# Cosine attention and a low-rank mixer with an MLP on one core: the combined blocks of the second MLP weight are built one unit earlier, in buffers that attention gives up

## The chip, the core and the metric

The kernel runs on one core of a Trainium2 chip. The metric is device time in microseconds (us); lower is better. TensorE (PE) multiplies matrices, VectorE (DVE), ScalarE (ACT) and GpSimd (POOL) work on elements, SyncE (SP) only starts transfers, as POOL does too. Every engine works through its own instructions strictly in the order in which they were written, and waits where an operand isn't ready.

## The reference

Inputs are q, k, v of 8 batches, 12 heads, 448 positions and 64 features. After the attention, its output is laid out as x with 448 rows and 768 columns for each batch:

```python
q_n = q / (norm(q) + 1e-06); k_n = k / (norm(k) + 1e-06)
attn = softmax(q_n @ k_n.T / tau)
x = (attn @ v).transpose(0, 2, 1, 3).reshape(B, S, H * D)
u = x + (x.T @ U @ V).T            # U: 448 x 32, V: 32 x 448
out = u + relu(u @ w_ch1) @ w_ch2  # w_ch1: 768 x 3072, w_ch2: 3072 x 768
```

The rest of this text calls the two weights w1 and w2. Multiplying by w1 is "up", multiplying by w2 is "down".

## The kernel before

**Tokens and units.** Two batches have 896 rows of u, which are seven tiles of 128 rows; four pairs of batches give 28 tiles. The MLP takes them in units. `PLAIN = [3, 4, 3, 4]` says that the first four units take 3, 4, 3 and 4 tiles and multiply in the ordinary way (`mlp`): up is 24 blocks of w1 times 6 steps, each a matmul of 128 columns per tile (L1294), then down is, for each tile and each half of the output columns, 24 matmuls of 384 columns (L1330). The other 14 tiles go in seven units of two tiles (`mlp_seven`). There, down uses seven block products in the place of eight: w2 is cut in 2 x 2 blocks, four combined blocks (`seven_weights`, L1014: T1, T2, T4, and one written over a block of w2) and as many combinations of the hidden values (`sums_of`, L1169 to L1172: S1, S2, an overwritten Q block, and S4) are formed by DVE subtractions, and each of seven products is 12 matmuls of 384 columns (L1217). The products are joined by DVE additions (L1233), one copy by ACT (L1238) and three additions by POOL (L1240). With `HALF = 2`, the first two of these seven units do an ordinary up for two tiles (24 x 6 matmuls of 256 columns, L1188), and the last five do up with seven products as well (`up_seven`, L1087, 252 matmuls of 128 columns), after `seven_rows` (L1046 to L1049) has formed combined blocks of w1.

**Attention** of batch b+1 and later runs beside the MLP units of earlier batches. For each batch, three loads of q and k (POOL's queue, L529) bring four heads each; DVE or ACT squares them (L581, L577), DVE sums (L585) and normalises (L653), SP starts transposing transfers (L668), PE forms scores (L714), ACT takes exponentials (L732), PE multiplies with v (L759), DVE divides into X (L788, L790). `stage0` then makes u from X: a projection (L866), a matmul with V (L921), and DVE additions of X (L931, L939). For batches from 2 on, u goes to DRAM (L964). A unit reads it back twice, transposed into uT (L816) and plain (L820).

**Buffers.** Rings hand out buffers in turn. Loads of q and k have 3 buffers (`r_ld`), normalised values 3 (`r_xn`), squares 3 (`r_sq`), transposed q and k 6 (`r_qkT`), projections 3 (`r_A`), u 4 for making (`r_us`) and 4 for reading back (`r_ur`). T1 and T2 lie over the load buffers and T4 over v of even batches and over the squares, so that they can be formed only when attention of the last batch no longer needs these.

**Order.** All operations are put in a list with durations that the author gave them, their dependencies, buffers and priorities. A planner (`Plan.run`) goes through time with these, and at each moment gives an engine the first ready operation: on PE by streams (attention before the MLP), on POOL by streams too, on DVE, ACT and SP by priority. The result is one fixed order for each engine. In the PE order, matmuls of the MLP thus stand between those of attention, and after the last batch's attention the MLP is alone.

Of the kernel before, what the change touches and what calls it, by code (L numbers as in the profile page):

```python
# [24 lines left out]
class Ring:  # L25
# [6 lines left out]
    def free_at(self, k=0):  # L32
        old = self.n + k - self.bufs
        return 0.0 if old < 0 else self.freed.get(old)

# [234 lines left out]
def kernel(  # L270
# [12 lines left out]
    nc = tc.nc  # L283
# [17 lines left out]
    PLAIN = [3, 4, 3, 4]  # L301
    HALF = 2
# [21 lines left out]
    def fixed_ring(tiles):  # L324
# [6 lines left out]
            for i in range(3)]  # L331
# [6 lines left out]
    r_ld, r_xn, r_attn, r_tail = fixed_ring(ld_t), fixed_ring(xn_t), fixed_ring(attn_t), fixed_ring(tail_t)  # L338
    sq_t = const.tile([128, 3, G // 2 * SC * D], BF, name="sq_all")
    r_sq = fixed_ring([sq_t[0:SCH, i].rearrange("p (h x) -> p h x", h=G // 2) for i in range(3)])  # L340
# [3 lines left out]
    qkT_t = const.tile([128, 6 * 2 * SC * SCH], BF, name="qkT")  # L344
    r_qkT = fixed_ring([qkT_t[:, 2 * SC * SCH * i:2 * SC * SCH * (i + 1)].rearrange("p (b s) -> p b s", b=2 * SC)
                        for i in range(6)])
    X_t = const.tile([128, 2 * 4 * C], BF, name="X_sb")
    r_X = fixed_ring([X_t[:, 4 * C * i:4 * C * (i + 1)].rearrange("p (t c) -> p t c", t=4) for i in range(2)])
    r_A = ring(3, [128, C], BF, "A_sb")
    u_t = const.tile([128, 8, C], BF, name="u_nat")  # L350
    r_us = fixed_ring([u_t[:, i, :] for i in range(4)])
    r_ur = fixed_ring([u_t[:, i, :] for i in range(4, 8)])
# [7 lines left out]
    views = [relu_t.bitcast(FP)[:, 0:4 * R + S + 4 * SC * D]] + [relu_t.rearrange("p (f n) -> p f n", f=NC)] * B  # L360
    r_relu = Ring(1, lambda i: views[min(i, B)])
# [22 lines left out]
    w_ = qkT_t.bitcast(FP)  # L384
    r_O3 = fixed_ring(O_2 + [w_[:, CH * i:CH * (i + 1)] for i in range(4)])
# [67 lines left out]
    pe_mlp = plan.stream("PE")  # L453
    pool_q = plan.stream("POOL")
# [345 lines left out]
    prev, first_v, made, u_adds = {}, {}, {}, {}  # L800
# [10 lines left out]
    def columns_of(tiles, uses=NC * CC):  # L811

        uT = Columns(128 * len(tiles), uses)
        us, ut = [], []
        for i, x in enumerate(tiles):
            ut.append(plan.add(Op("SP", 0.1, lambda i=i, x=x: nc.sync.dma_start_transpose(  # L816
                out=uT.tile[:, :, i * 128:(i + 1) * 128], in_=kept[x]),
                deps=[made[x]], acq=[uT.slot], prio=0, lat=("x", 0.05 * 48, 2.0))))
            u = Slot(r_ur, 2)
            u.back = plan.add(Op("SP", 0.1, lambda x=x, u=u: nc.sync.dma_start(out=u.tile, in_=kept[x]),  # L820
                                 deps=[made[x]], acq=[u], prio=1, lat=("x", 1.0, 2.0)))
            us.append(u)
        return us, uT, ut
# [30 lines left out]
    def stage0(b, X, muls):  # L854
# [39 lines left out]
        if not by_pe:  # L894
            tiles = range(4) if par == 0 else range(3, 7)
        us = [prev["u3"] if b > 1 and b % 2 and t == 3 else
              Slot(r_ur if b == 1 else r_us, 2 if b == 0 else 6 if by_pe else 1) for t in tiles]
        if not by_pe:
            prev["u3"] = us[-1]
# [7 lines left out]
        for z, (c0, c1) in enumerate(cols):  # L907
            for i, t in enumerate(tiles):
# [8 lines left out]
                for y, (AA, col) in enumerate(parts):  # L917
# [6 lines left out]
                        deps=[a_done[z]] if y == 0 else (), acq=[mm, u] if y == 0 else [],  # L924
                        rel=[AA]), pe_a if c1 < C else pe_av)

                def add(t=t, c0=c0, c1=c1, mm=mm, u=u, px=prev.get("X")):
                    w = c1 - c0
                    if t == 3 and not by_pe:
                        r = slice(64 * par, 64 * par + 64)  # L930
                        nc.vector.tensor_add(out=u.tile[r, c0:c1], in0=mm.tile[r, 0:w],  # L931
                                             in1=X.tile[r, 3 - 3 * par, c0:c1])
# [9 lines left out]
                rel = [mm, X] + ([prev["X"]] if t == 3 and by_pe else [])  # L942
# [15 lines left out]
        else:  # L958
            for i, t in enumerate(tiles):
                x, u = (b // 2, t), us[i]  # L960
                u_adds[x] = [adds[0, i], adds[1, i]] + u_adds.get(x, [])
                if t == 3 and par == 0:
                    continue
                made[x] = plan.add(Op("SP", 0.1, lambda x=x, u=u: nc.sync.dma_start(out=kept[x], in_=u.tile),  # L964
                                      deps=u_adds[x], rel=[u], prio=0, lat=("x", 1.0, 2.0)))
# [35 lines left out]
    stores, anchors = [], {}  # L1001

    def seven_weights(after, qk_free, v_free):

        B_ = w2_t.rearrange("p (j e) (h c) -> p j e h c", e=2, h=2)
        T1, T2 = [qk_t[:, HF * CH * i:HF * CH * (i + 1)].rearrange("p (j c) -> p j c", j=HF) for i in range(2)]
        flat = v_t[0].rearrange("p h c d -> p (h c d)")
        N4 = 9
        T4a = flat[:, 0:N4 * CH].rearrange("p (j c) -> p j c", j=N4)
        T4b = sq_t.rearrange("p i x -> p (i x)")[:, 0:(HF - N4) * CH].rearrange("p (j c) -> p j c", j=HF - N4)  # L1010
        ops = []

        def minus(out, a, b, deps):
            o = plan.add(Op("DVE", 0.06 + 3 * CH * 0.00053, lambda: nc.vector.tensor_sub(out, a, b), deps=deps, prio=3))  # L1014
            return o

        def t4(j0):
            return T4a[:, j0:j0 + 3] if j0 < N4 else T4b[:, j0 - N4:j0 - N4 + 3]
        by = {}
        for j0 in range(0, HF, 3):  # L1020
            x = slice(j0, j0 + 3)
            a = minus(T1[:, x], B_[:, x, 0, 1], B_[:, x, 0, 0], qk_free)
            c = minus(T2[:, x], B_[:, x, 1, 1], T1[:, x], [a])
            d = minus(t4(j0), B_[:, x, 1, 0], T2[:, x], [c, *v_free])
            e = minus(B_[:, x, 0, 1], B_[:, x, 1, 1], B_[:, x, 0, 1], [a, *after])
            for j in range(j0, j0 + 3):
                by[j] = {4: d, 5: a, 6: c, 7: e}
        right = {1: lambda j: B_[:, j, 0, 0], 2: lambda j: B_[:, j, 1, 0], 3: lambda j: B_[:, j, 1, 1],
                 4: lambda j: T4a[:, j] if j < N4 else T4b[:, j - N4], 5: lambda j: T1[:, j],
                 6: lambda j: T2[:, j], 7: lambda j: B_[:, j, 0, 1]}  # L1030
        return right, by

    def seven_rows(after, free):
# [3 lines left out]
        homes = [attn_all[:, N * n:N * (n + 1)] for n in range(8)] + [qkT_t[:, 4 * 2 * CH:4 * 2 * CH + N]]  # L1037
# [18 lines left out]
    def up_seven(tiles, relu, tops, ready, left, made_by, x_free):  # L1056
# [7 lines left out]
        def T(n):  # L1064
            return uT_t[:, CC * 256 + 384 * n:CC * 256 + 384 * (n + 1)].rearrange("p (i t) -> p i t", i=3)
# [3 lines left out]
        a = cols_(lambda: nc.vector.tensor_sub(T(0), U()[:, :, 0, 1], U()[:, :, 0, 0]), ut)  # L1069
# [48 lines left out]
        for k in (1, 6, 2, 7, 5, 3, 4):  # L1118
            for g in range(len(gs)):
# [25 lines left out]
                else:  # L1145
# [3 lines left out]
                    sums_of(gs[g], relu, ready, [x["r11"]], [x["r12"]], [x["r21"]], [x["r22"]], "DVE")  # L1149
# [3 lines left out]
    def relu_views():  # L1153
# [3 lines left out]
        return Q, [rl[:, 4 * HF + HF * i:4 * HF + HF * (i + 1)] for i in range(3)]  # L1157

    def sums_of(js, relu, ready, r11, r12, r21, r22, by="DVE"):

        Q, (S1, S2, S4) = relu_views()
        x = slice(js[0], js[-1] + 1)
        t = 0.15 + len(js) * 128 * 0.00053

        def sums(f, deps, by="DVE", prio=0.1):
            return plan.add(Op(by, t if by == "DVE" else 0.2 + len(js) * 128 * 0.0022, f, deps=deps, acq=[relu], prio=prio),
                            pool_q if by == "POOL" else None)
        side = nc.vector if by == "DVE" else nc.gpsimd
# [3 lines left out]
        d = sums(lambda: side.tensor_sub(S4[:, x], Q[:, x, 2], S2[:, x]), [c, *r21], by, prio=0.2)  # L1172
        for n, i in enumerate(js):
            ready[i] = {1: r11[n % len(r11)], 2: r21[n % len(r21)], 4: r22[n % len(r22)], 3: d, 5: a, 6: c, 7: e_}
# [388 lines left out]
```

## Time and profile before

| | us |
|---|---|
| median of 3 runs (lowest, highest) | 561.92 (561.49, 562.64) |
| the profiled execution, its own time | 560.98 |
| span of its profile | 559.2 |
| PE busy | 550.2 |
| DVE busy | 412.1 |
| ACT busy | 281.9 |
| POOL busy | 132.2 |

The span is the time from the first to the last instruction that the profile has; 1.8 us of the execution's own time lie outside it. A group row gives the source line, the engine, the operation, output and inputs, the count, the busy time in us, the mean duration of one in ns, and the idle time ahead of it. Busy time joins overlapping instructions, so that it can be less than count times mean. Durations of PE matmuls have the way through the array in them: what one costs in a row of them is the length of the row divided by the count, which the chain of work shows.

The stages by time: the fourth ordinary unit's up begins at 256.8 us and its down ends at about 345.4 us, with attention of batches 5 and 6 in between; the first seven-product unit runs from there to 386.9 us, with attention of batch 7; from 386.9 us on PE has the MLP alone; the last matmul ends at 554.9 us.

### The profile page before, as it was taken

What the parts mean: (1) busy time and instruction counts of PE and PEld (TensorE: products, weight loads), DVE (VectorE), ACT (ScalarE), POOL (GpSimd) and SP (SyncE); (2) the same over time, 40 slices, a digit from 0 to 9 for tenths busy, and PEclk for the clock granted to TensorE, in tenths of its full rate; (3) what the DMA queues carried; (4) which work ended last, traced back from release to release, by engine and by line L of the source; (5) the groups of instructions that cost most, each with busy time, mean ns of one, the idle gap of its engine ahead of it and who ended that gap; (6) DMA issues with size and microseconds to landing.
All of it is one profiled execution on the core that took longest, in us unless ns stands there. A gap on an engine that the chain in (4) does not pass through costs nothing.

```text
span 559.2 us, 13870 instructions
## 1 busy us (share of the span) xinstructions
PE 550.2 (98%) x5735; PEld 359.8 (64%) x5735; DVE 412.1 (74%) x940; ACT 281.9 (50%) x461; POOL 132.2 (24%) x165
## 2 busy tenths in 40 slices
PE   8999999999999999999999999999999999999996
PEld 6565566544655655565454666767869697878784
DVE  8989969999945797677684348849648686868683
ACT  7876645678545568545775533751414141414140
POOL 8526233153141050041222000010020303030212
PEclk9899999999999999999999999999999999999999
DMA  9999999699299595999469433014031212121201
GB/s 152 200 207 134 206 202 159 109 124 151 44 167 193 86 145 119 154 132 158 68 78 146 99 82 109 2 35 138 16 99 30 78 38 84 32 84 34 57 2 57
DMA packets 138720, 58.87 MB, mean 105 GB/s; under 512 B 98432, under 2 KB 138656, under 8 KB 138656
## 3 DMA queue, kind: packets, MB, share of 16 engines
q0 software_dynamic: 72352, 25.73, 41.6%
q1 hardware_dynamic: 66304, 32.25, 26.5%
q8 instruction: 45, 0.74, 0.5%
q14 instruction: 19, 0.16, 0.1%
HBM read 56.15 MB, written 15.14 MB: 127 GB/s over the span
## 4 chain that ended last, share of the span: by engine, by line
PE 94%; DVE 3%; ACT 1%; DMA 1%; issue 0%; DVEq 0%
PE bank L1330 20%; PE bank L1294 20%; PE bank L1217 17%; PE bank L1087 13%; PE bank L759 8%; PE bank L714 7%; PE bank L1188 6%; PE bank L921 2%; PE bank L507 1%; DVE qk_all L653 1%; ACT attn L727 1%; PE bank L866 1%; DVE ss L585 1%; DMA relu<-in_q_dram 1%; DVE X_sb L790 0%
## 5 line engine op out<-in xcount | busy, mean ns | idle before, releaser
L732 ACT ACTIVATE attn<-bank 128x896 bf16<-128x896 f32 (+1 forms) x163 | 139.9, 916 | 69.5 <-PE bank L714 68.9
L1330 PE MATMUL bank<-w_sb,relu 128*128 128x384 bf16 x672 | 121.0, 326 | 0.0
L1294 PE MATMUL bank<-uT,w_sb 128*128 128x384 bf16 (+1 forms) x576 | 119.8, 353 | 0.0
L1330 PEld LDWEIGHTS <-relu 128*128 128x128 bf16 x672 | 61.6, 98 | 44.7 <-issue 8.3
L1294 PEld LDWEIGHTS <-w_sb 128*128 128x128 bf16 x576 | 52.9, 98 | 51.9 <-issue 8.7
L1217 PEld LDWEIGHTS <-relu 128*128 128x128 bf16 x588 | 56.9, 98 | 37.4 <-issue 1.1
L585 DVE TENSOR_REDUCE ss<-sq_all 112x8 f32<-112x512 bf16 x96 | 61.5, 673 | 2.7 <-ACT sq_all L577 2.4
L759 PEld LDWEIGHTS <-attn 128*128 128x128 bf16 (+1 forms) x1536 | 54.5, 98 | 10.4 <-issue 3.6
L653 DVE TENSOR_TENSOR qk_all<-qk_all,inv 112x512 bf16<-112x512 bf16 x93 | 61.0, 682 | 0.2
L759 PE MATMUL bank<-v_nat,attn 128*128 128x65 bf16 (+1 forms) x1536 | 57.6, 193 | 0.9 <-DVE X_sb L790 0.4
L1217 PE MATMUL bank<-w_sb,relu 128*128 128x384 bf16 x336 | 58.1, 326 | 0.0
L714 PE MATMUL bank<-qkT 64*128 64x448 bf16 (+1 forms) x384 | 48.8, 359 | 1.1 <-ACT attn L727 0.6
L1317 ACT ACTIVATE relu<-bank 128x512 bf16<-128x512 f32 (+1 forms) x59 | 32.1, 545 | 32.4 <-PE bank L1294 32.2
L788 DVE RECIPROCAL rd<-bank 128x4 f32<-128x4 f32 x96 | 16.8, 176 | 42.0 <-PE bank L759 38.4
L529 POOL DMA_DIRECT2D qk_all<-in_q_dram x24 | 17.5, 731 | 120.4 <-issue 41.6
L552 POOL DMA_DIRECT2D v_nat<-in_v_dram x42 | 31.1, 752 | 59.8 <-PE bank L759 27.0
L1087 PE MATMUL bank<-uT,w_sb 128*128 128x128 bf16 x720 | 42.6, 219 | 0.0
L1087 PEld LDWEIGHTS <-w_sb 128*128 128x128 bf16 x720 | 41.0, 98 | 0.6
L790 DVE TENSOR_TENSOR X_sb<-bank,rd 128x256 bf16<-128x256 f32 x96 | 38.7, 413 | 1.3
L1124 ACT COPY X_sb<-bank 128x512 f32<-128x512 f32 x15 | 8.8, 587 | 60.4 <-PE bank L1087 59.5
L1240 POOL TENSOR_TENSOR relu<-relu,u_nat 128x384 f32<-128x384 f32 x3 | 5.0, 1663 | 129.8 <-ACT relu L1238 129.8
L577 ACT ACTIVATE sq_all<-qk_all 112x512 bf16<-112x512 bf16 x53 | 31.6, 629 | 4.3 <-DVE ss L585 4.2
(119 smaller groups left out, 700.8 us busy)
## 6 DMA issues: line engine op xcount, KB each, us to landing
qk_all<-in_q_dram POOLq DMA_DIRECT2D x23, 224.0 KB, 5.0
qk_all<-in_k_dram POOLq DMA_DIRECT2D x23, 224.0 KB, 6.5
w_sb<-in_moe_w_ch_dram POOLq DMA_DIRECT2D x4, 1152.0 KB, 19.2
w_sb<-in_moe_w_ch_dram POOLq DMA_DIRECT2D x8, 576.0 KB, 15.5
u<-u_nat SPq DMA_DIRECT2D x21, 192.0 KB, 2.3
u_nat<-u SPq DMA_DIRECT2D x21, 192.0 KB, 2.9
out_dram<-O_sb SPq DMA_DIRECT2D x14, 144.0 KB, 2.2
v_nat<-in_v_dram POOLq DMA_DIRECT2D x11, 168.0 KB, 9.2
```

The source lines that it names most:

```text
L585: lambda i=i, a0=a0, a1=a1, sq=sq: nc.vector.reduce_sum(ss.tile[:, i, a0:a1, :].rearrange("p h c -> p (h c)"), sq.tile[:, 0:a1 - a0, :].re ...
L653: nc.vector.tensor_mul(dst, src, sc)
L714: nc.tensor.matmul(out=out, lhsT=qkT.tile.rearrange("p b s -> p (b s)")[r, n0:n0 + w], rhs=qkT.tile[r, SC:2 * SC, :].rearrange("p c s -> p ...
L732: exps.append(plan.add(Op("ACT", act_t(2 * S, 0.08), lambda sc=sc, c=c, attn=attn: nc.scalar.activation(out=attn.tile[:, :, off:off + S] i ...
L759: nc.tensor.matmul(out=av.tile[:, t, 0:D + 1], lhsT=tail.tile[:, hh, 128 * t:128 * (t + 1)] if tail and j == SC - 1 else (attn if j < SC - ...
L790: muls.append(plan.add(Op("DVE", dve_t(256), lambda av=av, rd=rd, h=h: nc.vector.tensor_mul(X.tile[:, :, h * D:(h + 1) * D], av.tile[:, :, ...
L1087: o = plan.add(Op("PE", pe_t(128), lambda i=i, j=j, jj=jj: nc.tensor.matmul(out=mm.tile[:, 128 * jj:128 * jj + 128], lhsT=left[k](i, j), r ...
L1188: o = plan.add(Op("PE", pe_t(256), lambda j=j, e=e, cc=cc, mm=mm: nc.tensor.matmul(out=mm.tile[:, 256 * e:256 * e + 256], lhsT=w1_sb[:, cc ...
L1217: o = plan.add(Op("PE", pe_t(CH), lambda j=j: nc.tensor.matmul(out=mm.tile[:, 0:CH], lhsT=left[k](j), rhs=right[k](j), start=(first and j ...
L1294: o = plan.add(Op("PE", pe_t(n), lambda cc=cc: nc.tensor.matmul(out=mm.tile[:, 0:n], lhsT=w1_sb[:, cc, f * 128:(f + 1) * 128], rhs=uT.tile ...
L1317: nc.scalar.activation(out=relu.tile[:, f, 0:n], in_=mm.tile[:, 0:n], func=AF.Relu)
L1330: nc.tensor.matmul(out=mm.tile[:, 0:c1 - c0], lhsT=relu.tile[:, f, i * 128:(i + 1) * 128], rhs=w2_t[:, f, c0:c1], start=(f == 0), stop=(f ...
```

## The change

- `PLAIN` is `[3, 4, 3]` and `HALF` is 4. The four tiles that were the fourth ordinary unit become two units of two tiles with an ordinary up and seven products down. The number of units with seven products up stays five.
- The combined blocks of w2 have new homes: T1 in buffers of u, T2 in a load buffer, a normalised-value buffer and the second half of uT, T4 in a squares buffer, two transposed buffers, a projection buffer and the end of the hidden values' buffer. They are formed in 20 subtractions of two or three blocks each (16 before), the last of each group after the third ordinary unit's down.
- From batch 5 on (`WHOLE = 5`) attention has fewer buffers (`Shrink`): loads 2, normalised values 2, squares 2, transposed 4, projections 2. `Gone` tells the planner when the given-up ones are free. Reading u back has 2 buffers.
- u of batches from 2 on is made in place in X and stored from there. The tile that two batches share is stored by each in its half, so there are 24 stores for 21.
- S4 is no longer formed group by group beside the other sums. `last_sums` writes it over S1 in two subtractions of 768 columns, once product 5 has read S1; product 3 reads it.
- The POOL additions have a stream of their own (`pool_y`) ahead of the loads' stream, so that they can stand between loads.
- The combinations of the columns of u, the outputs of the last five units and one combined row block of w1 move to other parts of the same buffers.

```diff
-    PLAIN = [3, 4, 3, 4]
-    HALF = 2
+    PLAIN = [3, 4, 3]
+    HALF = 4
+    WHOLE = 5
...
-    r_ld, r_xn, r_attn, r_tail = fixed_ring(ld_t), fixed_ring(xn_t), fixed_ring(attn_t), fixed_ring(tail_t)
+    r_ld, r_xn, r_attn, r_tail = Shrink(ld_t, 3 * WHOLE, (0, 1)), Shrink(xn_t, NPAIR * WHOLE, (1, 2)), fixed_ring(attn_t), fixed_ring(tail_t)
...
+                    for i in range(6)], NPAIR * WHOLE, (2, 3, 4, 5))
...
+    A_t = const.tile([128, 3, C], BF, name="A_sb")
+    r_A = Shrink([A_t[:, i, :] for i in range(3)], WHOLE, (0, 1))
+    r_gone = Gone(r_ld, r_xn, r_sq, r_qkT, r_A)
-    r_us = fixed_ring([u_t[:, i, :] for i in range(4)])
-    r_ur = fixed_ring([u_t[:, i, :] for i in range(4, 8)])
+    r_ur = Shrink([u_t[:, i, :] for i in range(3)], 3, (0, 1))
+    r_u1 = fixed_ring([u_t[:, i, :] for i in range(3, 7)])
...
+    pool_y = plan.stream("POOL")
     pool_q = plan.stream("POOL")
...
-                        nc.vector.tensor_add(out=u.tile[r, c0:c1], in0=mm.tile[r, 0:w],
-                                             in1=X.tile[r, 3 - 3 * par, c0:c1])
+                    if not by_pe:
+                        r = slice(64 * par, 64 * par + 64) if t == 3 else slice(0, 128)
+                        x = X.tile[r, t - 3 * par, c0:c1]
+                        nc.vector.tensor_add(out=x, in0=mm.tile[r, 0:w], in1=x)
...
+        runs = {1: [(u_t.rearrange("p i c -> p (i c)")[:, 2 * C:], 0, HF)],
+                2: [(qk_t[:, 2 * QC:2 * QC + 8 * CH], 0, 8), (uT_t[:, CC * 256:], 8, HF)],
+                4: [(sqk_t[:, 2 * SQ:2 * SQ + 6 * CH], 0, 6), (A_t[:, 2, :], 6, 8),
+                    (relu_t[:, 72 * 128:84 * 128], 8, HF)]}
...
+        for j0, j1 in ((0, 3), (3, 6), (6, 8), (8, 10), (10, 12)):
+            a = minus(T1, B_[:, x, 0, 1], B_[:, x, 0, 0], n, downs[1])
+            c = minus(T2, B_[:, x, 1, 1], T1, n, [a, tops[1][-1] if j0 == 10 else tops[2][-1] if j0 == 8 else None], [gone])
+            d = minus(T4, B_[:, x, 1, 0], T2, n, [c, *downs[1]], [gone])
+            e = minus(B_[:, x, 0, 1], B_[:, x, 1, 1], B_[:, x, 0, 1], n, [a, *after])
...
-        d = sums(lambda: side.tensor_sub(S4[:, x], Q[:, x, 2], S2[:, x]), [c, *r21], by, prio=0.2)
...
+    def last_sums(ready, done):
+        Q, (S1, S2) = relu_views()
+        for j0 in range(0, HF, 6):
+            x = slice(j0, j0 + 6)
+            d = plan.add(Op("DVE", 0.15 + 6 * 128 * 0.00053, lambda x=x: nc.vector.tensor_sub(
+                S1[:, x], Q[:, x, 2], S2[:, x]), deps=[done, *(ready[j][6] for j in range(j0, j0 + 6))], prio=-0.55))
...
         p5 = product(5, c, True, False)
+        last_sums(ready, p5)
```

## Prediction

> **What bounds the kernel now.** I read the page first, then the chain of work in order of time, then busy time by stage, then single groups and transfers.
>
> ```profile
> span 559.2 us, 13870 instructions
> PE 550.2 (98%) x5735; PEld 359.8 (64%) x5735; DVE 412.1 (74%) x940; ACT 281.9 (50%) x461; POOL 132.2 (24%) x165
> ...
> PE   8999999999999999999999999999999999999996
> ...
> DVE  8989969999945797677684348849648686868683
> ...
> PE 94%; DVE 3%; ACT 1%; DMA 1%; issue 0%; DVEq 0%
> ```
>
> PE is busy 98% of the span, and its slices fall below 9 only at the two ends; 94% of the chain that ended last is PE. Its losses are about 5 us at the start and 4.3 us after the last matmul, both outside the change. So the time is PE's list of matmuls, as long as nobody makes PE wait. The price of each kind is read from unmixed rows of the chain (start, length, what):
>
> ```profile
> 290.07 2.81 PE bank L1294 x13
> ...
> 386.92 15.72 PE bank L1188 x144
> 402.64 13.65 PE bank L1217 x84
> 416.29 14.07 PE bank L1087 x252
> ...
> 541.24 13.66 PE bank L1217 x84
> ```
>
> Length by count: 216 ns for a 512-column up matmul (2.81/13), 109.2 ns for a 256-column one (15.72/144), 162.5 ns for a 384-column down one (13.65/84), 55.8 ns for 128 columns. The stages that the change touches, by window (PE, PEld, DVE, ACT, POOL busy, granted PE clock):
>
> ```profile
> 257.00:300.00 43.00, 43.00 (x392) 21.21 (x391) 31.11 (x71) 31.27 (x51) 9.71 (x14) 1.00 0.76 96
> 300.00:345.00 45.00, 45.00 (x454) 26.74 (x452) 21.86 (x54) 18.82 (x23) 0.00 (x0) 1.00 0.43 106
> 345.00:386.90 41.90, 41.90 (x475) 29.60 (x474) 30.96 (x74) 21.24 (x29) 2.65 (x3) 1.00 0.20 53
> ```
>
> PE never idles there, its clock is full, and DVE has 35 us to spare in the first 88.
>
> **The change part by part.** *Matmuls.* The fourth ordinary unit goes: 144 up matmuls of 512 columns (144 x 0.216 = 31.1 us) and 192 down matmuls (192 x 0.1625 = 31.2 us). Two seven-product units come: 288 up matmuls of 256 columns (288 x 0.1092 = 31.45 us) and 168 down matmuls (168 x 0.1625 = 27.3 us). Sum: 58.75 - 62.3 = -3.55 us. The changed program has 120 PE matmuls more (288 + 168 - 144 - 192), and its counts of all other kinds are unchanged.
>
> Here a rule speaks against the change. The Trainium skill, "TensorE: Matmul & The Clock Gate", section "Back-to-back issue gap", says that in a stream of weight load and matmul pairs the spacing is about 81 ns at 128 columns and 131 ns at 512, since both instructions count. A line through these gives an estimate of 98 ns at 256 and 114 ns at 384: up would go from 144 x 0.131 = 18.9 to 288 x 0.098 = 28.2 us, down from 21.9 to 19.2, and the change would cost 6.6 us. The rows of this trace say 55.8, 109.2 and 216 ns, so width alone sets the price and the halved width costs 0.3 us. I take the rows: same program, same pairs. Mixed with attention, the 256-column row is 1.96 us for 17 (115 ns), with a switch of kind in it; the 512-column row mixed in the same way, 2.05 us for 9 (228 ns), pays the same. For both I leave it out.
>
> *DVE work.* Removed: 8 output additions (0.551 us each), 23 S4 subtractions (15 x 0.452, 8 x 0.354), 16 weight subtractions (0.748 each): 26.0 us. Added: 12 output additions (0.553), 24 sums of three blocks (0.354), 18 S4 subtractions of 768 columns and 12 weight subtractions of the same width (0.55, between 0.354 at 384 and 0.748 at 1152), 8 weight subtractions of 1152 (0.748), 3 relus more on DVE (0.69, and 3 fewer on ACT): 6.6 + 8.5 + 9.9 + 6.6 + 6.0 + 2.1 = 39.7 us. So DVE gets 13.7 us more.
>
> ```profile
> L1172 DVE TENSOR_TENSOR relu<-relu 128x512 bf16<-128x512 bf16 x15 | 6.4, 452 | 0.0
> ...
> L1014 DVE TENSOR_TENSOR qk_all<-w_sb,qk_all 128x1152 bf16<-128x1152 bf16 x4 | 3.0, 748 | 0.0
> ...
> L1233 DVE TENSOR_TENSOR O_sb<-bank,O_sb 128x384 f32<-128x384 f32 x20 | 10.6, 553 | 12.7 <-PE bank L1217 9.5 <-POOL O_sb L1240 1.8 <-issue 1.2
> ```
>
> Nearly all of it falls where unit four was, and the weight subtractions, at 336 to 358 us before, now stand mostly beside the third unit's down, just ahead of it. In the changed program's order the two new units hold 158 DVE instructions; at the means above, each less the 0.07 us by which it overlaps its neighbour, they are 65 us beside 78 us of PE work. That is hidden on the whole. Its densest place, the 24 us of PE work from there into the first new unit's first relus, holds 26 us of DVE work, so DVE is 1 to 2 us late there. Most of that is weight subtractions that nobody waits for, but DVE relus stand behind them; PE reuses their bank 1.2 us after their place in the order, of which a relu takes 0.69. If the cover is gone, PE loses up to 0.8 us once or twice: 0 to 1.5 us, and I take 0.3. (The same density before, 17 us of DVE work in 16 us at the old weight subtractions, cost PE nothing.)
>
> *S4 over S1.* In an up-and-down unit with ordinary up, product 4 (12 x 0.1625 = 1.95 us) stands between product 5, the last reader of S1, and product 3, the reader of S4. After product 5 DVE now does two S4 subtractions and then the addition that frees product 3's bank: about 0.15 + 0.55 + 0.5 + 0.55 = 1.75 us, formerly 0.7. It is covered with 0.2 us to spare; without cover 0.3 us in each of four units. I take 0.1 in all. The five units with seven products up have products 7 and 2 there, 3.9 us: nothing.
>
> *POOL.* Six additions more, three of them ahead of loads of q, k and v. Their durations differ:
>
> ```profile
> 405.26 0.91 POOL L1240 TENSOR_TENSOR relu<-relu,u_nat 128x384 f32<-128x384 f32 x1 [32.33 <-ACT relu L1238]
> ...
> 432.98 3.17 POOL L1240 TENSOR_TENSOR relu<-relu,u_nat 128x384 f32<-128x384 f32 x1 [24.36 <-ACT relu L1238]
> ```
>
> The second ran while DVE did subtractions between SBUF buffers one after another (431.6 to 435.4 us). The Trainium skill, "SBUF — State Buffer", section "Who interferes with whom", says that a DVE tensor-tensor operation with both inputs in SBUF contends with GpSimd's reads. By the short row the first addition is ready 0.3 + 0.48 + 0.1 + 0.91 = 1.8 us after product 1, and the DVE addition that needs it comes after product 6, at 1.95 us: nothing lost. By the long row it is ready at 4.05, the DVE addition ends at 4.7, and product 7 would start at 3.9: 0.8 us in each new unit. DVE does attention there, most of it reading PSUM or slower, with gaps, so I stay near the short row: 0.1 us. Loads behind the additions are held about 3 us, no more than their buffer holds them anyway (they wait on a normalisation 0.6 us ahead of them in the order).
>
> *Fewer attention buffers, moved transfers.*
>
> ```profile
> qk_all<-in_q_dram POOLq DMA_DIRECT2D x23, 224.0 KB, 5.0
> ...
> u_nat<-u SPq DMA_DIRECT2D x21, 192.0 KB, 2.9
> ...
> qkT<-qk_all SPq DMA_TRANSPOSE x36, 4.5
> ```
>
> With four transposed buffers the shortest lead of a transpose over the scores that use it is 10 us of PE work, formerly 19; it lands in 4.5 us, 7.1 at most from batch 4 on: hidden. With two load buffers the shortest lead of a q load over its first square is 3.5 us, and twice ACT will wait 1 to 2.5 us there. The next instruction of ACT that PE needs stands 6 us on: hidden, and 1 us each if not. Three more stores of u (0.37 us on SP) and two read-back buffers (load in 2.9 us, needed 14 us later, behind the up) are hidden. X is held 2.3 us longer by its stores, and its next writer comes a batch later. The other moved homes change no work. Price 0.
>
> Sum: -3.55 + 0.3 + 0.1 + 0.1 = about -3.1 us. The profiled execution has 559.2 us of span and 1.8 around it, so its like would take 557.9; the median of the runs lies 0.9 above that execution, and the median after should be 561.92 - 3.1 = 558.8 us.
>
> **The rivals.** *DVE becomes the bound in the new units.* For it: 26 us of DVE work in 24 of PE work, and a relu slack of about 0.4 us. Against it: the average there is 83%, and equal density cost nothing before. With POOL's long row in both new units (1.6) or repeated waits for relus, 1 to 3 us are lost: 559.4 to 561.4 us.
>
> *Attention starves on two load buffers; slower.* Place: the squares of each third of batches 5 to 7, nine in all. A load may start only once the third two before is normalised; if landing takes the 7.3 us of the slowest one after 195 us rather than 5.0, the square is 3.8 us late, and with it the normalisation, the next load and at last the scores, as the chain has only two buffers to absorb it. Nine times 0.4 us eats the whole gain; nine times 1.0 us gives 561.92 - 3.55 + 9 = 567.4 us. Against it: seven of nine thirds have longer leads, and PE has MLP matmuls to do between.
>
> *Narrower up matmuls are dearer than the lone row.* It decides at (62.3 - 27.3)/288 = 121.5 ns; at the 6.6 us of the rule the time is 568.5. The trace's 109 to 115 speak against it.
>
> *The new waits are all covered*: -3.55 and half a microsecond of scatter, 557.5 to 558.4.
>
> **How the numbers follow.** About 0.2% (1.1 us) is what a measurement of this kernel can tell from no change. Likeliest case, including the fully covered one, 0.78: 557.6 to 559.6. DVE as bound 0.16, three quarters of it still faster by more than 0.2% (0.12), the rest the same (0.04). Starving 0.05, of it 0.04 slower and 0.01 the same. Dear matmuls 0.01, slower. So faster 0.90, same 0.05, slower 0.05. The range, 557.5 to 561.0, takes the likeliest case whole and most of the DVE one.
>
> **What would show it.** Right: PE busy falls to about 547 us, 288 more matmuls of 256 columns at 109 to 115 ns, 168 more of 384, no waits of PE over 0.5 us between 250 and 390 us, the last stage alone as before (13.65 and 14.07 us rows), the tail still 4.3 us. Wrong: idle PE between 225 and 300 us with DVE relus or sums as releaser (DVE case), scores waiting for transposes (starving), or a 256-column row over 120 ns.

## The result, and the profile after

| | before | after |
|---|---|---|
| median of 20 runs each (lowest, highest), us | 561.48 (560.21, 562.64) | 558.97 (557.61, 561.05) |
| span of the profiled execution, us | 559.2 | 557.1 |
| PE busy, us | 550.2 | 547.6 |
| DVE busy, us | 412.1 | 425.0 |
| PE matmuls | 5735 | 5855 |

The ratio of the times is 0.9959, with an interval of 0.9949 to 0.997. So the change took 2.5 us (1.7 to 2.9) from the time, where 3.1 had been forecast; 558.97 lies in the range on record.

First come lines of the page of the changed kernel: the span, busy time of each engine, and the slices of PE and DVE.

```profile
span 557.1 us, 14190 instructions
...
PE 547.6 (98%) x5855; PEld 371.8 (67%) x5855; DVE 425.0 (76%) x969; ACT 282.2 (51%) x461; POOL 134.5 (24%) x171
...
PE   8999999999999999999999999999999999999997
...
DVE  8889969999955685479889878545978685858583
```

PE has 120 matmuls more and is still busy for 2.6 us less. DVE is busier by 12.9 us, and its full slices have moved to where the two new units are.

The next lines are the windows of the changed kernel (stretch, length, then busy PE, PEld, DVE, ACT, POOL, granted PE clock, DMA share, GB/s). The first four together cover the place where most of the weight subtractions now stand, the two new units and the rest of attention; the fifth lies in the last five units, those with seven products up.

```profile
240.00:257.00 17.00, 17.00 (x144) 9.59 (x141) 16.33 (x34) 4.58 (x7) 0.72 (x2) 1.00 0.36 98
257.00:300.00 43.00, 43.00 (x492) 31.32 (x493) 38.13 (x92) 25.79 (x43) 13.77 (x18) 1.00 1.05 127
300.00:345.00 45.00, 45.00 (x508) 32.26 (x505) 36.50 (x88) 28.10 (x45) 13.25 (x17) 1.00 0.89 118
345.00:386.90 41.90, 41.90 (x453) 29.50 (x451) 22.07 (x56) 22.75 (x30) 2.65 (x3) 1.00 0.32 67
420.00:540.00 120.00, 119.15 (x1483) 96.85 (x1481) 88.48 (x173) 34.39 (x58) 16.04 (x12) 1.00 0.22 54
```

DVE is at 16.33 of 17, 38.13 of 43 and 36.50 of 45 us, and PE is without a gap in all of these. The only one of these stretches in which PE stands still is one that the change was not expected to touch: 0.85 us are missing in the last five units. The waits of PE name it; from 40 us on this is the whole list (who waits for whom, us in total, times, longest):

```profile
PE bank L1274 <- DVE relu L1218: 0.8, 1, 0.8
```

Three landmarks in PE's order split the difference between the two traces: the start of the first up matmul of the first unit, of the first matmul with seven products up, and of the last matmul.

| | first up to seven-up, us | seven-up to last matmul, us |
|---|---|---|
| before | 377.8 | 138.4 |
| after | 374.5 | 139.5 |

The middle gave 3.3 us. The last five units, whose matmuls are the same in number and kind, took 1.0 us back. That is a little more than the 0.85 us for which the profile shows PE idle, since a 384-column matmul is recorded with 326 ns on the mean and costs 162.5 ns in a row. What is left of the difference lies in the start, which varies by over 1 us from execution to execution (first up matmul at 38.3 us before, at 38.7, 39.6 and 39.3 in three executions of the changed kernel).

What happens at the wait is seen in the timeline of the changed kernel, in the first of the last five units (start, length, engine and line, operation, operands, count, and in brackets the idle time before it and its releaser). L1217 to L1219 are the sums S1 (an addition), S2 and the overwritten Q block (subtractions); L1297 is a POOL addition.

```profile
426.83 1.97 ACT L1166 ACTIVATE relu<-relu 128x512 bf16<-128x512 bf16 x3 [2.05 <-DVE relu L1160]
428.06 0.69 DVE L1194 TENSOR_SCALAR relu<-relu 128x512 bf16<-128x512 bf16 x3
428.82 0.76 DVE L1217 TENSOR_TENSOR relu<-relu 128x512 bf16<-128x512 bf16 x2
...
429.50 0.75 DVE L1218 TENSOR_TENSOR relu<-relu 128x512 bf16<-128x512 bf16 x2
430.03 0.99 POOL L1297 TENSOR_TENSOR relu<-relu,u_nat 128x384 f32<-128x384 f32 x1 [24.04 <-ACT relu L1295]
430.17 1.13 DVE L1217 TENSOR_TENSOR relu<-relu 128x512 bf16<-128x512 bf16 x1
...
431.22 1.13 DVE L1219 TENSOR_TENSOR relu<-relu 128x512 bf16<-128x512 bf16 x1
432.28 1.13 DVE L1218 TENSOR_TENSOR relu<-relu 128x512 bf16<-128x512 bf16 x1
...
433.46 0.82 PE L1274 MATMUL bank<-uT,relu 128*128 128x384 bf16 x4 [0.85 <-DVE relu L1218]
```

Three sums of 512 columns take 1.13 us each, as long as three POOL additions stand beside them. The last is S2 of the last group, and product 6 on PE waits for it. In the next unit of the same trace the same instructions go otherwise:

```profile
458.07 0.75 DVE L1218 TENSOR_TENSOR relu<-relu 128x512 bf16<-128x512 bf16 x2
458.70 2.58 POOL L1297 TENSOR_TENSOR v_nat<-v_nat,u_nat 128x384 f32<-128x384 f32 x1 [25.58 <-ACT v_nat L1295]
458.75 0.42 DVE L1217 TENSOR_TENSOR relu<-relu 128x512 bf16<-128x512 bf16 x1
```

Here a sum takes 0.42 us and the POOL addition 2.58, and PE loses nothing. So in one unit POOL holds DVE up, in the other four DVE holds POOL up. Which of the two it is turns on a tenth of a microsecond: POOL's addition starts 0.14 us ahead of the next DVE sum in the first case and 0.05 us ahead in the second.

The trace also shows where that tenth comes from. It is not POOL that is early in the first unit; the sums are late. There the first of these sums starts at 428.82 us, when the last of ACT's three relus ends (426.83 + 1.97 = 428.80), 0.07 us after DVE's own relus (428.75). In the next unit it starts at 457.40, right behind DVE's own relus and 0.15 us before ACT's end (457.55). Counted from the start of product 1 on PE (427.25 and 455.99), the sums begin at 1.57 us in the first unit and at 1.41 in the next, POOL at 2.78 and 2.71.

### The profile page after: what moved, and what is told of

Read it like the earlier page. It is cut to its first block, busy times and chain, and to the rows that moved or that the text cites. A ratio compares the mean times of both kernels' runs of the same rounds, so it can differ in the third digit from the quotient of the medians.

```text
span 557.1 us, 14190 instructions
## 1 busy us (share of the span) xinstructions
PE 547.6 (98%) x5855; PEld 371.8 (67%) x5855; DVE 425.0 (76%) x969; ACT 282.2 (51%) x461; POOL 134.5 (24%) x171
## 5 line engine op out<-in xcount | busy, mean ns | idle before, releaser
L1274 PEld LDWEIGHTS <-relu 128*128 128x128 bf16 x756 | 72.2, 98 | 50.0 <-issue 3.6
L1389 PE MATMUL bank<-w_sb,relu 128*128 128x384 bf16 x480 | 86.7, 326 | 0.0
L1353 PE MATMUL bank<-uT,w_sb 128*128 128x384 bf16 (+1 forms) x432 | 85.9, 344 | 0.0
L1274 PE MATMUL bank<-w_sb,relu 128*128 128x384 bf16 x432 | 75.7, 326 | 0.0
L1245 PE MATMUL bank<-uT,w_sb 128*128 128x256 bf16 x576 | 69.0, 273 | 0.0
L634 DVE TENSOR_REDUCE ss<-sqk 112x8 f32<-112x512 bf16 x96 | 62.2, 674 | 3.9 <-ACT sqk L626 3.6
L1389 PEld LDWEIGHTS <-relu 128*128 128x128 bf16 x480 | 44.1, 98 | 31.7 <-issue 5.7
L1353 PEld LDWEIGHTS <-w_sb 128*128 128x128 bf16 x432 | 39.8, 98 | 35.8 <-issue 6.1
L1245 PEld LDWEIGHTS <-w_sb 128*128 128x128 bf16 x576 | 54.8, 98 | 11.7 <-issue 4.2
L702 DVE TENSOR_TENSOR qk_all<-qk_all,inv 112x512 bf16<-112x512 bf16 x93 | 62.5, 696 | 0.1
L763 PE MATMUL bank<-sqk 64*128 64x448 bf16 (+1 forms) x384 | 48.8, 359 | 1.0 <-ACT sqk L1411 0.6
L1138 PEld LDWEIGHTS <-w_sb 128*128 128x128 bf16 x720 | 41.0, 98 | 0.6
L839 DVE TENSOR_TENSOR X_sb<-bank,rd 128x256 bf16<-128x256 f32 x96 | 38.7, 414 | 1.2
L626 ACT ACTIVATE sqk<-qk_all 112x512 bf16<-112x512 bf16 x54 | 32.5, 629 | 13.8 <-DVE ss L634 12.0
L1255 ACT ACTIVATE relu<-bank 128x512 bf16<-128x512 f32 x33 | 19.7, 597 | 26.6 <-PE bank L1245 23.2
```

Of the source, the lines that this page charges most:

```text
L626: nc.scalar.activation(out=y, in_=x, func=AF.Square)
L634: lambda i=i, a0=a0, a1=a1, sq=sq: nc.vector.reduce_sum(ss.tile[:, i, a0:a1, :].rearrange("p h c -> p (h c)"), sq.tile[:, 0:a1 - a0, :].re ...
L702: nc.vector.tensor_mul(dst, src, sc)
L763: nc.tensor.matmul(out=out, lhsT=qkT.tile.rearrange("p b s -> p (b s)")[r, n0:n0 + w], rhs=qkT.tile[r, SC:2 * SC, :].rearrange("p c s -> p ...
L839: muls.append(plan.add(Op("DVE", dve_t(256), lambda av=av, rd=rd, h=h: nc.vector.tensor_mul(X.tile[:, :, h * D:(h + 1) * D], av.tile[:, :, ...
L1138: o = plan.add(Op("PE", pe_t(128), lambda i=i, j=j, jj=jj: nc.tensor.matmul(out=mm.tile[:, 128 * jj:128 * jj + 128], lhsT=left[k](i, j), r ...
```

## The experiments

After the result two theories stood. *Port*: the 1.0 us came from POOL's additions getting in ahead of DVE's sums where both work between SBUF buffers. *Parts*: S4's new place, or attention's fewer buffers, or the narrower up matmuls cost something that the change's other gains cover. Each run was compared with the kernel before on the same chip, whose median was 561.26 in the runs 1 to 7 and 561.62 in the last two.

### 1. POOL additions behind the sums, in the planner's list

```diff
-            out=y_.tile, in0=s1.tile, in1=u.tile[:, c0:c0 + CH]), deps=[cp, u.back], acq=[y_], rel=[s1, u]), pool_y)
+            out=y_.tile, in0=s1.tile, in1=u.tile[:, c0:c0 + CH]), deps=[cp, u.back] + ([ready[HF - 1][7]] if up is not None else []), acq=[y_], rel=[s1, u]), pool_y)
```

> The changed kernel, but in the five units with seven products up the POOL additions also wait for the last group's sums on DVE; the order of every engine is unchanged. Port theory (the 0.85 us for which PE waits at 433 us is DVE's sums held back by a POOL addition that began between two of them): the 1.13 us subtractions go back to 0.42 us, PE's wait of 0.8 us is gone, the POOL additions all take 0.9 to 1.3 us, and the time is 558.97 - 0.85 = about 558.1 us. Rival (the gain fell short because DVE is too full in the two new units, or because the start differs): no change, 559.0 us.

Measured: 559.66 us (558.01 to 560.60), ratio 0.9971 (0.9959 to 0.9983). The dependency entered only the planner's list. The order of every engine came out as before, and what an instruction waits for on the chip follows from its data, so this is the changed kernel once more. It tells nothing of the theories, but it is a second measurement: the same single wait of 0.8 us at the same place, 374.9 and 139.5 us between the landmarks, and the sums at 1.13 to 1.14 us each.

### 2. S4 over S1 alone

The kernel before, with S4 formed by two subtractions into S1 after product 5, and nothing else of the change:

```diff
-        d = sums(lambda: side.tensor_sub(S4[:, x], Q[:, x, 2], S2[:, x]), [c, *r21], by, prio=0.2)
...
+            d = plan.add(Op("DVE", 0.15 + 6 * 128 * 0.00053, lambda x=x: nc.vector.tensor_sub(
+                S1[:, x], Q[:, x, 2], S2[:, x]), deps=[done, *(ready[j][6] for j in range(j0, j0 + 6))], prio=-0.55))
...
+        last_sums(ready, p5)
```

> The kernel before with S4 written over S1 in two subtractions after product 5, and nothing else of the change. If leaving S4 out of the row of sums is what lets a POOL addition in between DVE's sums: a PE wait of about 0.8 us on a sum in one or more of the five last units, up to 4 us in all, 562 to 563 us beside the 561.5 of before. If S4 has no part in it: 561.5 us, no such wait. The step S4 over S1 of the prediction: 0.1 us in all, no wait of PE for the addition that frees product 3's bank.

Measured: 561.84 us (561.13 to 563.03), ratio 1.0011 (1.0005 to 1.0018), so 0.6 us slower. The waits of PE in this kernel have one line that the kernel before has not:

```profile
PE bank L1226 <- DVE O_sb L1242: 0.4, 1, 0.4
```

It is in one of the two seven-product units with ordinary up that this kernel has: product 3 waits for the DVE addition that stands behind the S4 subtractions. That is the stall that the prediction priced at 0.3 us "without cover", so its mechanism is real. In the last five units the sums stay at 0.345 to 0.422 us. S4's place therefore does not by itself bring the wait of 0.8 us; and in the whole change, where this wait of 0.4 us is not in the list, its other order covers it.

### 3. Fewer attention buffers alone

The kernel before, with the rings of loads, normalised values, squares, transposed values and projections shrunk from batch 5 on, but the combined blocks of w2 left in their old homes:

```diff
+    WHOLE = 5
...
-    r_ld, r_xn, r_attn, r_tail = fixed_ring(ld_t), fixed_ring(xn_t), fixed_ring(attn_t), fixed_ring(tail_t)
+    r_ld, r_xn, r_attn, r_tail = Shrink(ld_t, 3 * WHOLE, (0, 1)), Shrink(xn_t, NPAIR * WHOLE, (1, 2)), fixed_ring(attn_t), fixed_ring(tail_t)
```

> The kernel before with attention's buffers cut from batch 5 on as in the change, with nothing gained from them. Prediction: price 0, 561.5 us, no PE wait over 0.5 us. Starving rival: PE waits for scores or transposes in batches 5 to 7, 564 us or more.

Measured: 569.20 us (568.93 to 570.11), ratio 1.0146 (1.0129 to 1.0162), so 8 us slower. No scores wait for a transposing transfer here either. The wait is another one. The waits of PE in this kernel:

```profile
PE bank L1239 <- DVE qk_all L1036: 4.2, 3, 3.2
```

The longest of the three in its timeline:

```profile
374.32 1.12 PE L1239 MATMUL bank<-qk_all,relu 128*128 128x384 bf16 x3 [3.16 <-DVE qk_all L1036]
```

The products wait for the combined blocks of w2 themselves. In the old homes these can be formed only when the last batch's attention no longer needs the buffers there; with fewer buffers that attention comes later (its last score matmul starts at 383.9 us, before at 373.7), and the subtractions run from 366.5 to 382.3 us in place of 336.3 to 358.7. After the wait PE's clock is low as well (windows of this kernel, columns as above):

```profile
370.00:375.00 5.00, 1.84 (x37) 1.29 (x34) 5.00 (x8) 0.83 (x2) 1.65 (x2) 0.85 0.00 0
375.00:380.00 5.00, 4.61 (x44) 2.70 (x42) 4.96 (x12) 2.54 (x3) 0.00 (x0) 0.50 0.02 3
```

From 40 us on PE stands still for 4.4 us (4.2, and 0.2 elsewhere). By these two windows the clock is at half for about 6.5 us, in which PE works for between 5 and 6; that costs some 3 us more by estimate. Together these are most of the 8 us.

So the rings' price of 0 belongs to the change as a whole. In it, attention is late too (its last score matmul starts at 381.8 us), but nothing of the MLP waits for the end of attention any more, because the combined blocks lie in the given-up buffers and are formed by 261.8 us, ahead of the first new unit's products, which begin at 278.0. Fewer buffers with the old homes cost 8 us, and the new homes are the buffers given up: the two parts pay only together.

### 4. Narrower up matmuls alone

The kernel before, with the fourth ordinary unit cut in two of two tiles, so that its 144 up matmuls of 512 columns become 288 of 256:

```diff
-    PLAIN = [3, 4, 3, 4]
+    PLAIN = [3, 4, 3, 2, 2]
```

> The kernel before with the fourth unit as two units of two tiles, ordinary up and ordinary down: 288 up matmuls of 256 columns in the place of 144 of 512, the same down matmuls. By the rows of the trace (109.2 and 216 ns): +0.35 us, 561.8 us, the four-tile stretch of PE longer by that. By the rule of 81 to 131 ns for a pair: +9 us, 570.8 us. With switches of kind dearer for narrow matmuls (115 against 216 ns): +2 us, 563.5 us.

Measured: 565.95 us (562.37 to 568.16), ratio 1.0075 (1.0047 to 1.0103), so 4.7 us slower, by far more than width by the rows (0.3 us), but all six executions lie below the 570.8 us of the rule that the prediction weighed. In the trace most of it is not width. The waits of PE in this kernel have one long one:

```profile
PE bank L1294 <- ACT relu L1317: 2.6, 1, 2.6
```

ACT's timeline ahead of it:

```profile
261.54 1.15 ACT L577 ACTIVATE sq_all<-qk_all 112x512 bf16<-112x512 bf16 x2 [2.02 <-DMA qk_all<-in_k_dram]
```

A square on ACT waits 2.02 us for a load of k. A relu stands behind it in ACT's order, and PE stands still until the relu has freed its bank. Then the clock falls; PE's timeline has the 17 matmuls after the gap in 3.3 us (268.71 less 265.39, where the next kind begins), 195 ns each:

```profile
263.82 0.49 PE L1294 MATMUL bank<-uT,w_sb 128*128 128x256 bf16 x3 [2.63 <-ACT relu L1317]
264.14 1.43 PE L759 MATMUL bank<-v_nat,attn 128*128 128x65 bf16 x32
265.39 3.39 PE L1294 MATMUL bank<-uT,w_sb 128*128 128x256 bf16 x17
268.71 0.74 PE L714 MATMUL bank<-qkT 64*128 64x448 bf16 x6
```

The sum is 2.6 for the gap, 17 x 0.086 = 1.5 for these matmuls and 0.3 for width, together 4.4 of the 5.2 us by which the way from the first up matmul to the first seven-up one is longer than before (383.0 against 377.8 us). This execution took 566.41 us, and not all are like it: four of the six took 565.8 to 568.2 at a mean granted clock of 0.994, the other two 563.44 and 562.37 at 0.997. That the two were spared the low clock, or the gap, is likely and not shown, since only one execution was traced. The run thus says nothing against the price of a 256-column matmul, and a good deal about the second rival: one late load, with ACT's order behind it, costs 4 us where it happens. The unit differs from the change's new units in its relus too (twice as many, half as wide), so it stands for the mechanism only.

### 5. The copy of product 1 behind the sums

The changed kernel, with the copy that releases POOL's additions given to DVE, behind the sums of the same unit, in the last five units:

```diff
-        cp = plan.add(Op("ACT", 0.42, lambda: nc.scalar.copy(out=s1.tile, in_=a.tile[:, 0:CH]),
-                         deps=[p1, *after], acq=[s1], prio=-0.5))
+        if up is None:
+            cp = plan.add(Op("ACT", 0.42, lambda: nc.scalar.copy(out=s1.tile, in_=a.tile[:, 0:CH]),
+                             deps=[p1, *after], acq=[s1], prio=-0.5))
+        else:
+            cp = plan.add(Op("DVE", 0.5, lambda: nc.vector.tensor_copy(out=s1.tile, in_=a.tile[:, 0:CH]),
+                             deps=[p1, *after, *(ready[j][k] for j in range(HF) for k in (6, 7))], acq=[s1], prio=-0.5))
```

> The changed kernel, but in the five units with seven products up the copy of product 1, which the POOL additions read, is made by DVE behind its sums instead of by ACT beside them, so that no POOL addition can begin between the sums. Port theory (PE waits 0.8 us at 433 us because a POOL addition got in between two sums and each of the next three subtractions then took 1.13 us): all sums at 0.42 us, no such wait, POOL additions at about 0.9 us each, and 0.85 us less than the changed kernel, about 558.1 to 558.5 us on this chip. Rival (the sums are late in the first of these units for another reason, such as ACT): the wait stays, 559.0 to 559.7 us.

> The changed kernel with the copy of product 1 in the last five units made by DVE behind its sums, once more, for a direct comparison. Port theory: 0.85 us less than the changed kernel on the same chip, 558.2 to 558.8 us, and from the first to the last matmul of the last five units 138.5 us, not 139.4. Rival: the two agree within 0.3 us.

Measured: 559.01 us (557.43 to 559.47), ratio 0.9954 (0.9941 to 0.9967), and again beside the changed kernel: 558.14 us (557.08 to 559.36), ratio 0.994 (0.9926 to 0.9954). In both traces no wait of PE is left in the last five units, and these take 138.4 us, as in the kernel before. The first median alone would not have told: 559.01 lies where the rival was expected (559.0 to 559.7), not at 558.1 to 558.5. The traces decide, and with them the comparison on one chip (559.16 less 558.14 us, see 8). The window of the last five units in the first of the two runs:

```profile
420.00:540.00 120.00, 120.00 (x1499) 97.89 (x1497) 90.66 (x178) 33.37 (x56) 11.24 (x12) 1.00 0.22 54
```

The first of these units in its timeline:

```profile
431.67 0.42 DVE L1218 TENSOR_TENSOR relu<-relu 128x512 bf16<-128x512 bf16 x1
...
433.30 0.95 POOL L1301 TENSOR_TENSOR relu<-relu,u_nat 128x384 f32<-128x384 f32 x1 [26.47 <-DVE relu L1299]
...
435.27 1.06 DVE L1123 TENSOR_TENSOR uT<-uT 128x384 bf16<-128x384 bf16 x1
```

The sums are at 0.42 us, and the POOL addition, which now begins behind them, at 0.95. PE gains the 0.85 us of the window. The contention is not gone, it has moved: beside the later POOL additions a combination of the columns of u (L1123) takes 1.06 us (0.35 in the changed kernel, at 435.51 us, with no POOL addition beside it), but PE doesn't wait for that one.

### 6. The sums 0.12 us later

The changed kernel, with two writes of four elements (0.06 us each on DVE) ahead of the first sum of each of the last five units; they do no work that anything needs:

```diff
+        def first():
+            if len(js) == 4 and js[0] == 0:
+                nc.vector.memset(idle_t, 0.0)
+                nc.vector.memset(idle_t, 0.0)
+            nc.vector.tensor_add(S1[:, x], Q[:, x, 1], Q[:, x, 3])
```

> The changed kernel with two tiny DVE writes (about 0.06 us each) ahead of the first group's sums in each of the five units with seven products up. Port theory, with who comes first deciding (the POOL addition begins 0.53 us after the second pair of sums where PE waits, 0.63 us after it where it doesn't): now POOL gets in first in all five units, sums of 1.13 us in all, and PE waits about 0.9 us in each: up to 3.6 us more than the changed kernel, 562.5 us. Rival: 0.13 us of DVE work in each unit are hidden, no more than 0.1 us.

Measured: 562.80 us (562.70 to 564.35), ratio 1.0033 (1.0021 to 1.0045): 1.5 us slower than the kernel before. The waits of PE in this kernel:

```profile
PE bank L1280 <- DVE relu L1224: 4.1, 5, 0.8
```

The window of its last five units:

```profile
420.00:540.00 120.00, 116.70 (x1440) 93.95 (x1438) 91.00 (x176) 33.46 (x56) 12.49 (x12) 1.00 0.22 54
```

The first two of the five places in its timeline:

```profile
430.36 0.96 POOL L1303 TENSOR_TENSOR relu<-relu,u_nat 128x384 f32<-128x384 f32 x1 [24.04 <-ACT relu L1301]
430.46 1.13 DVE L1222 TENSOR_TENSOR relu<-relu 128x512 bf16<-128x512 bf16 x1
...
459.00 1.04 POOL L1303 TENSOR_TENSOR v_nat<-v_nat,u_nat 128x384 f32<-128x384 f32 x1 [25.58 <-ACT v_nat L1301]
459.18 1.13 DVE L1222 TENSOR_TENSOR relu<-relu 128x512 bf16<-128x512 bf16 x1
```

One wait of 0.8 us has become five, one for each unit. POOL's first addition now starts 0.10 to 0.19 us ahead of the next sum in the five units, and each time it is DVE that is held up, in the second unit by an addition with the same operands as the one that was held up itself in the changed kernel. In the first unit the two writes change little: the sums wait for ACT there anyway. The last five units take 143.4 us from the first seven-up matmul to the last matmul, 4.0 us more than in the changed kernel, or 1.0 us for each of the four units that were free of the wait. Together with run 5, this settles the port theory: taking POOL's additions away from the sums takes the wait away, and moving the sums by 0.12 us brings it to all five units.

### 7. The POOL additions back in the loads' stream

```diff
-            out=y_.tile, in0=s1.tile, in1=u.tile[:, c0:c0 + CH]), deps=[cp, u.back], acq=[y_], rel=[s1, u]), pool_y)
+            out=y_.tile, in0=s1.tile, in1=u.tile[:, c0:c0 + CH]), deps=[cp, u.back], acq=[y_], rel=[s1, u]), pool_q)
```

> The changed kernel with the POOL additions back in the stream of the loads, behind the last batch's loads. The first new unit's additions then come only after the loads of batch 7, and what needs them is planned later. Prediction's view of POOL (six additions more, hidden): the stream of their own is what lets the new units run inside attention; without it PE gets waits on those additions or the planner moves the attention matmuls: 560 to 565 us. If it doesn't matter: 559.0 to 559.7 us.

Measured: 586.47 us (584.09 to 587.11), ratio 1.0441 (1.0421 to 1.0461). The longest of PE's waits in this kernel:

```profile
PE bank L1274 <- DVE O_sb L1290: 5.5, 1, 5.5
```

A window of it:

```profile
300.00:345.00 45.00, 35.41 (x343) 20.53 (x343) 32.75 (x78) 20.35 (x28) 10.95 (x15) 0.69 0.72 104
```

POOL ahead of its first addition:

```profile
315.05 0.70 POOL L578 DMA_DIRECT2D qk_all<-in_q_dram  x1 [15.70 <-DVE qk_all L702]
...
323.76 2.65 POOL L1297 TENSOR_TENSOR O_sb<-relu,u_nat 128x384 f32<-128x384 f32 x3
```

The first POOL addition starts at 323.8 us (281.5 in the changed kernel), behind loads that wait for their buffers, one of them for 15.7 us. DVE's addition waits for it, PE for DVE, and the clock is at 0.69 in that window. So the stream of its own, to which the prediction gave no price, is worth about 27 us here (the ratios 1.0441 and 0.9959 of 561 us). How much of that is the additions' own wait, the other waits that came with the new order, or the low clock, the run does not separate.

### 8. The changed kernel again

> The changed kernel as it is, beside the next one on one chip. Two profiles of it have the same PE wait of 0.8 us at the same place in the first unit with seven products up, so a third has it too: 559.0 to 559.7 us.

Measured, beside the second run of the version of 5: 559.16 us (558.40 to 559.49), ratio 0.9953 (0.9941 to 0.9965); the same wait of 0.8 us, 374.5 and 139.5 us between the landmarks.

**The best version** is that of 5. On one chip it took 558.14 against 559.16 us, and its trace has 1.0 us less in the last five units. The intervals of the two ratios overlap (0.9926 to 0.9954, and 0.9941 to 0.9965), so the gain over the changed kernel is shown by the traces, and only likely by the times. Against the kernel before it took 2.2 us less in the first run and 3.5 in the second, by medians.

## Why the prediction was right, and which term was off

- **Matmuls, -3.55 us: right.** Counts came out as listed (5855), PE is busy for 547.6 us (about 547 forecast), and 4.1 us follow the last matmul (4.3 before). The unmixed row of 256 columns in the changed kernel's timeline is 28 matmuls from 396.24 us to the next kind at 399.30, 109.3 ns each; the row of before had said 109.2, and the rule that was weighed beside it (the Trainium skill, "TensorE: Matmul & The Clock Gate", "Back-to-back issue gap"; 98 ns by the estimate made from it) is not borne out in this kernel. The end alone is as before (chain of the changed kernel; start, length, what):

```profile
442.09 14.07 PE bank L1138 x252
456.16 13.65 PE bank L1274 x84
...
553.00 0.56 DVE O_sb L1290
```

- **The middle gave 3.3 us of 3.55.** Between 40 and 400 us the trace has no wait of PE that accounts for the other 0.25. It is not located. Three traces of the changed kernel agree to within 0.4 us (374.5, 374.9 and 374.5), but of the kernel before there is only one.
- **DVE work, 0.3 us: nothing of it seen.** DVE got 12.9 us more (13.7 forecast) and stands at 16.33 of 17 and 38.13 of 43 us in its densest stretches, but PE waited for no relu. The rival of DVE as the bound did not occur.
- **S4 over S1, 0.1 us: nothing of it seen in the changed kernel**, and 0.4 us once where it was done alone (2).
- **Fewer attention buffers, 0: right, with a condition.** ACT does wait for a load once, 1.6 us (forecast: twice, 1 to 2.5), and PE does not notice. The prediction argued this from the leads of transfers alone. It left out that the end of attention moves 8 us back (last score matmul at 381.8 us, 373.7 before), which costs nothing only since the combined blocks no longer stand behind that end (3). The starving rival did not occur, but 4 shows how near its mechanism is.
- **POOL, 0.1 us: this term was mis-sized; it measured 1.0 (0.85 of it as idle time of PE).** It failed in two ways. It priced only the two new units, where the additions fall beside attention, and put the last five at nothing, though the row of 3.17 us stood in one of them and the change shifts the order around it. And it took that row as the sole form of the contention: POOL held up by DVE. The other outcome, DVE held up by POOL, stood in the same trace beside the very row of 0.91 us that was read as free of contention. DVE's next subtraction, begun less than 0.06 us after that POOL addition, took 1.67 us, where its like took 0.95 just before:

```profile
403.64 0.95 DVE L1049 TENSOR_TENSOR w_sb<-w_sb 128x1536 bf16<-128x1536 bf16 x1
...
405.31 1.67 DVE L1049 TENSOR_TENSOR w_sb<-w_sb 128x1536 bf16<-128x1536 bf16 x1
```

  PE did not wait for that subtraction, so nothing in PE's time told of it. The section of the Trainium skill that was cited, "Who interferes with whom" of "SBUF — State Buffer", has both outcomes: "Issue order, not op shape, decides who blocks." By the starts in these traces that holds for the sums where POOL leads by 0.10 us or more, not at 0.05. With both outcomes as the ends of the range, the same three sums at 1.13 in place of 0.42 us would have been three times 0.7 less their slack on PE, in up to five units; run 6 shows this dearer end at 5.0 us, 1.0 in each unit. It turns the change into a loss.

The sum with the measured terms is -3.3 + 1.0 = -2.3 us, against -2.5 measured by the medians. The mechanism, PE's list of matmuls with the new waits covered, was right. That the total came so near is in part luck: 0.5 us had been allowed for stalls in three places where none came, and a stall of twice that size came where none had been priced. A tenth of a microsecond more on DVE would have brought it five times (6).

## What to carry to other kernels

Where two engines slow each other down, a slow row of one of them in the trace shows one outcome only: look beside the fast rows for the other engine's slow one, price that outcome too, and ask of every unit whose order shifts, also of those that the change doesn't touch, which of the two will be held up. When buffers are taken from a stage, look not only at its transfers but at what waits for the stage's end. Waits of PE as long as the two here (2.6 and 3.2 us) are to be priced with the low clock that followed them, and not by their own length.

## What the runs showed of the hardware

- **Which engine is held up turns on less than a tenth of a microsecond.** POOL additions of 384 columns in 32 bit stood beside DVE additions and subtractions of 512 columns in 16 bit, all between SBUF buffers. Where POOL started 0.10 to 0.19 us ahead of the next sum, three sums took 1.13 us each (0.42 alone); where it started 0.05 us ahead, POOL's addition took 2.58 us (0.91 where it was not held up). So starting first by the trace was not enough for POOL at 0.05 us. In the kernel before, POOL got through with a lead of less than 0.06 us over a subtraction of 1536 columns; whether the limit depends on the shape, the runs don't tell. The one that got through lost little (POOL's first additions took 0.96 to 1.04 us), and sums 0.12 us later cost 4.0 us over the last five units.
- **The tenth is no chance, but its cause is only read.** POOL's lead in the first of the five units was 0.13 to 0.14 us in all three profiled executions of the changed kernel, and 0.05 in the next unit. That the first sum waits there for ACT's last relu is read from the trace; no run tested it.
- **A gap of PE of 2.6 us was followed by more than 3 us of low speed.** In the traced execution of 4, 17 matmuls of 256 columns took 195 ns each after the gap, 109 elsewhere; in 3 the granted clock was 0.50 in the five microseconds from 375, after a wait of 3.16 us that ended at 374.3. In 6, after five waits of 0.8 us, it stayed at 1.00.
